# Bucketed attention and two MLPs on one core: four-element reciprocal, GpSimd spreads and value splits, a 128-row bucket-code product, transfers from SyncE

## Chip, cores and metric

One core of a Trainium2 chip runs the whole program. The metric is the device time of one execution in microseconds. Engines are called by the profile's names: PE is TensorE's matmul stream and PEld its weight loads, DVE is VectorE, ACT is ScalarE, POOL is GpSimd, SP is SyncE.

## What is computed

```python
q_bits = (np.einsum('bhsd,dk->bhsk', q, proj) > 0)          # B, H, S, D = 2, 8, 768, 64; 6 bits
mask = q_bucket[:, :, :, None] == k_bucket[:, :, None, :]   # bucket = bits as a number
scores = scale * np.matmul(q, k.transpose(0, 1, 3, 2))
scores = np.where(mask, scores, -1000000000.0)
scores = scores - np.max(scores, axis=-1, keepdims=True)
attn = np.exp(scores)
attn = attn / (np.sum(attn, axis=-1, keepdims=True) + 1e-09)
x = np.matmul(attn, v)                  # heads side by side: 1536 rows of 512
gate = 1.0 / (1.0 + np.exp(-(x @ w_gate)))
x = gate * (x @ w_val) @ w_out          # 512 -> 1536 -> 512
h = x @ w_in                            # 512 -> 2048
g = np.where(h >= 1, h, np.where(h <= -1, 0.0, (h + 1) ** 2 / 4))
out = g @ w_out2                        # 2048 -> 512
```

## The kernel before

The 16 heads are taken as eight pairs (`seq`, L395), the attention of a pair as 12 units (`Unit`): two heads times six tiles of 128 queries. Each unit is one step `kk` of a loop that is written out by hand in `manual_schedule` (L398, L484), so the program's order is the order in each engine's queue. A unit computes scores for 128 queries against 768 keys in PSUM (`QK`, L303, four matmuls), takes the negated row maximum on VectorE (`MAX`, L311), the exponential with its row sum on ScalarE (`EXP`, L315), transposes the 768 columns back through TensorE in pieces of four (`Flip.T`, L341, tile `pt`, two PSUM buffers), and splits each piece into a high f16 part on ScalarE (`HI`, L347) and a low f16 part on VectorE (`LO`, L350). A `pt` buffer is free again only when its `LO` has read it. Every fourth unit closes a group: `ST1` (L318) scales the four row sums, `ST2` (L322) takes their reciprocal on VectorE, spread over 4x64 columns as it is read, into `rb`; two steps later `norm` transposes `rb` on TensorE (L355, tile `r`) and the product with V begins (`pv`, L381, 60 matmuls a group, cut into four pieces). `evac` (L388) multiplies product and reciprocal on VectorE.

V stays exact by a split: `split_v` (L367, L369) makes two residuals of it on VectorE, half a head pair at a time, at steps 1, 3, 5 and 6 of a pair (`VST`, L469); every product with V reads them.

Beside the units of one pair runs the preparation of the next (`Prep`): transposes of q and k (L208, L209, tile `T`), copies and residuals (L212, L216), the hash projections (`z`, L225), their signs (`bits`, L229) and a product with a table of bucket codes (`xp`, L235) that yields a one-hot of the bucket. The table `code` has 56 rows, the signs 56 rows. Five moves between partitions (L281) for each of q and k, and the loads of later q, k and v (`load_qk`, `load_v`), are DMAs from GpSimd's queue, in program order; GpSimd does nothing else in the loop. SyncE issues the first loads and moves and, later, all weights. The last pair has no preparation beside it.

After the attention come the two MLPs, in which TensorE works from weights that SyncE loads (L103).

Of the kernel before, what the change touches and what calls it, by code (L numbers as in the profile page):

```python
# [7 lines left out]
F32 = mybir.dt.float32  # L8
F32R = mybir.dt.float32r
F16 = mybir.dt.float16  # L10
BF16 = mybir.dt.bfloat16
I64 = mybir.dt.int64
U32 = mybir.dt.uint32
AF = mybir.ActivationFunctionType
ALU = mybir.AluOpType
# [11 lines left out]
def lsh_attention_glu_act(ctx, tc, q, k, v, proj, w_gate, w_val, w_out1, w_in2, w_out2, ident_d, code_d, out):  # L27
    nc = tc.nc
# [4 lines left out]
    HN = S // 2  # L33
# [10 lines left out]
    const = ctx.enter_context(tc.tile_pool(name="const", bufs=1))  # L44
# [6 lines left out]
    ZR = 32 + 4 * NB  # L51
    ZW = 72
    Z0 = 32 + 2 * NB
    code_f = const.tile([ZR, 2, 2, 128], F32, name="code_f")
    code = const.tile([ZR, 2, 2, 128], BF16, name="code")
    cst = const.tile([128, 4], F32, name="cst")
    pz = const.tile([128, 2, Z0 + ZW], F32R, name="pz")

    def constants():
        nc.vector.memset(pz.bitcast(F32), 0.0)  # L60
        for i, c in enumerate((-TINY, -2.0 * BIG, -float(NB), 0.5)):
            nc.vector.memset(cst[:, i:i + 1], c)
        nc.scalar.dma_start(ident, ident_d)
        nc.gpsimd.dma_start(proj_sb[E], proj)
        nc.gpsimd.dma_start(proj_sb[O], proj)
        nc.gpsimd.dma_start(code_f, code_d)
        for e, r in ((0, E), (1, O)):
            cs = slice(Z0 + e * NB, Z0 + (e + 1) * NB)
            nc.vector.tensor_copy(pz[r, 0, cs], proj_sb[r])
            nc.vector.tensor_tensor(out=pz[r, 1, cs], in0=proj_sb[r], in1=pz[r, 0, cs].bitcast(F32), op=ALU.subtract)  # L70

    def f(ap):
        return ap.bitcast(F32)
# [77 lines left out]
    with ExitStack() as actx:  # L151
        ap = actx.enter_context(tc.tile_pool(name="attn", bufs=2))
# [1 line left out]
        DMA = nc.gpsimd  # L154
        NAT, PR = {}, {}

        def load_qk(b, p, eng=nc.gpsimd):
            nat = []
            for j, src in enumerate((q, k)):
                t = ap.tile([128, 2, NI * D], F32, tag="nat", bufs=4, name=f"n{j}_{b}_{p}")  # L160
                nat.append(t)
            NAT[b, p] = nat
            eng.dma_start(nat[0], q[b, 2 * p:2 * p + 2].rearrange("h (p i) d -> p h (i d)", i=NI))
            for e in range(2):
                eng.dma_start(nat[1][:, 1 - e], k[b, 2 * p + e].rearrange("(p i) d -> p (i d)", i=NI))

        def load_v(b, p, eng=nc.gpsimd):
            vr = ap.tile([128, 2, NI * D], F32, tag="vr", name=f"vr_{b}_{p}")
            eng.dma_start(vr, v[b, 2 * p:2 * p + 2].rearrange("h (p i) d -> p h (i d)", i=NI))
            VR[b, p] = vr  # L170

        def top(t, i):
            return t.bitcast(BF16).rearrange("p h (s t) -> p h s t", t=2)[:, :, :, i]
# [4 lines left out]
        SG = 4  # L178

        class Prep:  # L180
# [44 lines left out]
                    nc.tensor.matmul(self.z_ps[0:ZW, 0:HN], lhsT=pz[:, c, s:s + ZW], rhs=self.t4[j][t][:, n * HN:(n + 1) * HN], start=(m == 0), stop=(m == len(steps) - 1))  # L225

            def bits(self):
                self.bt = ap.tile([ZR, HN], BF16, tag="bits", bufs=1, name=f"bits_{self.b}_{self.p}")
                nc.scalar.activation(out=self.bt, in_=self.z_ps[0:ZR, 0:HN], func=AF.Sign, bias=cst[0:ZR, 0:1])  # L229

            def xp(self, j, n=None):
                self.x_ps = self.bank(n, f"xp{j}_{self.b}_{self.p}")
                for a in range(2):
                    if n is None or n == a:
                        nc.tensor.matmul(self.x_ps[:, a] if n is None else self.x_ps, lhsT=code[:, a, j, :], rhs=self.bt, start=True, stop=True)  # L235

            def Hot(self, j, dst, r, n=None):
                dst = self.sb(dst, n)[r]
# [38 lines left out]
            def copy(self, j, m):  # L277
                tU, tW, tH, tN = self.t4[j]
                s0, s1 = self.rows(j)
                dst, src = ((tN[O], tU[s0]), (tU[s0], tW[s1]), (tW[s1], tN[O]), (tN[E], tH[E]), (tH[E], tU[s1]))[m]  # L280
                nc.gpsimd.dma_start(f(dst), f(src))  # L281

            def done(self):
                A = [(t[2], t[3]) for t in self.t4]
# [3 lines left out]
        class Unit:  # L288
# [16 lines left out]
            def MAX(self):  # L305
                self.c = self.n % SG
                if self.c == 0:
                    self.st = ap.tile([128, 3, SG], F32, tag="st", bufs=4, name=f"st_{self.u}")
                else:
                    self.st = un[self.n - 1].st  # L310
                nc.vector.tensor_reduce(out=self.st[:, 0, self.c:self.c + 1], in_=self.sc[:, :, 0:HN], op=ALU.max, axis=AX.XY, negate=True)  # L311
# [6 lines left out]
                nc.vector.tensor_scalar(out=self.st[:, 2], in0=self.st[:, 1], scalar1=1e-9, scalar2=PSCALE, op0=ALU.add, op1=ALU.mult)  # L318

            def ST2(self):  # L320
                self.rb = ap.tile([128, 4, 64], F32, tag="rb", name=f"rb_{self.u}")
                nc.vector.reciprocal(out=self.rb, in_=self.st[:, 2].unsqueeze(2).broadcast_to([128, 4, 64]))  # L322

        class Flip:
            def __init__(self, n):
# [34 lines left out]
        def split_v(b, p, h, k):  # L360
            vr = VR[b, p]
            if h == 0 and k == 0:
                VS[b, p] = ap.tile([128, 2, NI * D], F32, tag="vs", name=f"vs_{b}_{p}")
            vs = VS[b, p]
            hs = slice(k, k + 1)
            if h == 0:
                nc.vector.tensor_tensor(out=vs[:, hs], in0=vr[:, hs], in1=top(vr, 1)[:, hs], op=ALU.subtract)  # L367
            else:
                nc.vector.tensor_tensor(out=top(vs, 0)[:, hs], in0=vs[:, hs], in1=top(vs, 1)[:, hs], op=ALU.subtract)  # L369

        def pv(b, p, g, PT):
            vr, vs = VR[b, p], VS[b, p]
# [22 lines left out]
        seq = [(b, p) for b in range(B) for p in range(NP)]  # L395
        UP = 2 * NI

        with tc.manual_schedule():  # L398
            ws0, wraw = [], []

            def load_w(w, t):
                raw = ap.tile([128, 2 * S], I64, tag="PT", bufs=3, name=f"wr_{t}_0")[:, 0:512]
                nc.sync.dma_start(raw.rearrange("p (a n) -> p a n", a=KC), col_chunk(w, 0))
                wraw.append(raw)
# [24 lines left out]
            fw = first_weights()  # L429

            load_qk(*seq[0], nc.sync)
            constants()
            load_w(w_gate, "g")
            load_qk(*seq[1], nc.gpsimd)
            pp, p1 = Prep(*seq[0]), Prep(*seq[1])
            for j in range(2):
                pp.T(j)
# [10 lines left out]
            for j in range(2):  # L448
                pp.swap(j)
            load_v(*seq[0], nc.sync)  # L450
            load_w(w_val, "v")
            nc.vector.tensor_copy(code, code_f)
            pp.bits()
            hold = []
            for j in range(2):
# [28 lines left out]
            for kk in range(-2, NU + DLY + 7):  # L484
# [12 lines left out]
                st = 0 <= kk < NU and kk % SG == SG - 1  # L497
# [28 lines left out]
                if 0 <= pi < len(seq) and m in VST:  # L526
                    split_v(*seq[pi], *VST[m])
# [27 lines left out]
                if nxt and pm == 4 and pj + 2 < len(seq):  # L555
                    load_qk(*seq[pj + 2])
                if 0 <= pi < len(seq) - 1 and m == 9:
                    load_v(*seq[pi + 1])
# [5 lines left out]
                if 0 <= kk - GV0 < 2:  # L564
                    n = kk - GV0
# [165 lines left out]
```

## Time and profile before

| | |
|---|---|
| median of 3 runs | 908.0 us (907.74 to 908.94) |
| the profiled execution | 907.66 us, span 905.8 us |
| busy, share of the span | PE 96%, PEld 87%, DVE 66%, ACT 53%, POOL 6% |
| chain that ended last | PE 70%, DVE 13%, DMA 5%, ACT 5%, issue 5% |
| granted clock of TensorE, mean | 0.987 |

A busy share says how long an engine was occupied, not that it set the pace. Ends of matmuls are modelled, so waits of PE are read best as the distance between the starts of two neighbours, compared with the same two neighbours where nothing held them up. The attention takes the first 330 us of the span, the MLPs the rest.

### The profile page before, as it was taken

To read this page: it belongs to the slowest core of one execution; us is meant where nothing else is said; L and a number is where in the kernel's file an instruction comes from. 1 tells how busy PE (TensorE), PEld (TensorE's weight loads), DVE (VectorE), ACT (ScalarE), POOL (GpSimd) and SP (SyncE) were. 2 spreads that over 40 slices of the span, in tenths; PEclk is the share of its full clock that TensorE was granted. 3 is DMA by queue.
4 is the path that set the end of the run, shared out by engine and by line. 5 is a ranking of instruction groups with operands and counts; after the bars stand their busy time and mean duration, and the time that the engine had idled before them with its cause. 6 is when DMAs were issued, how large, how long until landed. Compare 5 with 4: busy or idle time off the path is not lost.

```text
span 905.8 us, 14442 instructions
## 1 busy us (share of the span) xinstructions
PE 871.1 (96%) x5840; PEld 785.9 (87%) x5840; DVE 601.0 (66%) x1000; ACT 476.8 (53%) x903; POOL 57.0 (6%) x106
## 2 busy tenths in 40 slices
PE   6799999999999889999999999999999999999998
PEld 4587877778777679999999999999999998999996
DVE  4788888888888867453455879599984444444343
ACT  4667677676776654222222435454765555555443
POOL 2212112121111000000000000000000000000000
PEclk9799999999999999999999999999999999999999
DMA  7324323243221005212122543044430001000001
GB/s 211 88 58 106 92 71 97 58 109 89 71 63 45 1 1 164 70 59 81 47 73 87 169 139 118 23 140 149 129 95 1 1 1 43 27 1 1 1 1 71
DMA packets 33811, 64.49 MB, mean 71 GB/s; under 512 B 3060, under 2 KB 24660, under 8 KB 33744
## 3 DMA queue, kind: packets, MB, share of 16 engines
q1 hardware_dynamic: 27616, 41.16, 14.6%
q0 software_dynamic: 5984, 22.34, 9.8%
q8 instruction: 46, 0.75, 0.3%
q14 instruction: 21, 0.17, 0.1%
q10 hardware_dynamic: 144, 0.07, 0.0%
HBM read 45.27 MB, written 3.15 MB: 53 GB/s over the span
## 4 chain that ended last, share of the span: by engine, by line
PE 70%; DVE 13%; DMA 5%; ACT 5%; issue 5%; POOL 1%; SPq 0%; ACTq 0%; POOLq 0%; DVEq 0%
PE p L123 5%; PE p L125 5%; PE p L124 5%; PE o L646 5%; PE o L647 5%; PE o L645 5%; DVE st L311 4%; PE O L381 4%; PE pg L125 4%; PE pg L123 4%; PE pv L123 4%; PE pv L125 4%; PE pv L124 4%; PE pg L124 3%; PE pt L341 3%
## 5 line engine op out<-in xcount | busy, mean ns | idle before, releaser
L350 DVE SCALAR_TENSOR_TENSOR PT<-pt,PT 128x512 f16<-128x512 f32 x144 | 98.5, 684 | 48.5 <-ACT PT L347 48.2
L315 ACT ACTIVATE P<-sc,st 128x768 f32<-128x768 f32 x96 | 86.4, 900 | 49.4 <-DVE st L311 45.8
L341 PE MATMUL pt<-ident,P 128*128 128x128 f32 x576 | 94.4, 284 | 11.1 <-DVE PT L350 10.3
L347 ACT ACTIVATE PT<-pt 128x512 f16<-128x512 f32 x144 | 85.8, 596 | 25.4 <-PE pt L341 25.2
L341 PEld LDWEIGHTS pt<-ident,P 128*128 128x128 f32 x576 | 67.5, 143 | 29.1 <-DVE PT L350 18.1
L311 DVE TENSOR_REDUCE st<-sc 128x1 f32<-128x768 f32 x96 | 89.7, 934 | 0.4 <-PE sc L303 0.4
L381 PE MATMUL O<-PT,vs 128*64 128x256 f16 x864 | 89.2, 279 | 0.0
L123 PE MATMUL p<-yh,wh_i 128*128 128x384 f32 x256 | 86.1, 336 | 0.2 <-DVE yl L602 0.2
L125 PE MATMUL p<-yh,wl_i 128*128 128x384 f32 x256 | 86.0, 336 | 0.0
L124 PE MATMUL p<-yl,wh_i 128*128 128x384 f32 x256 | 85.8, 335 | 0.0
L381 PE MATMUL O<-PT,vr 128*64 128x256 f16 x576 | 75.9, 280 | 2.0 <-ACT x_3h L136 2.0
L647 PE MATMUL o<-wh_o,gl 128*128 128x512 f32 x192 | 75.3, 392 | 0.0
L646 PE MATMUL o<-wl_o,gh 128*128 128x512 f32 x192 | 75.2, 392 | 0.0
L645 PE MATMUL o<-wh_o,gh 128*128 128x512 f32 x192 | 74.7, 389 | 0.0
L629 DVE SCALAR_TENSOR_TENSOR g<-p,t 128x384 f32<-128x384 f32 x64 | 35.4, 553 | 48.3 <-ACT t L627 48.3
L149 DVE SCALAR_TENSOR_TENSOR h<-sg,pv 128x384 f32<-128x384 f32 x48 | 26.4, 550 | 56.2 <-PE pv L125 50.0
L147 ACT ACTIVATE sg<-pg 128x384 f32<-128x384 f32 x48 | 23.4, 487 | 70.2 <-PE pg L125 68.4
L631 DVE TENSOR_TENSOR gl<-g,gh 128x384 fp32r<-128x384 f32 x64 | 35.6, 557 | 31.5 <-ACT gh L630 31.5
L626 ACT ACTIVATE t<-p,cst 128x384 f32<-128x384 f32 x64 | 36.6, 572 | 36.8 <-PE p L125 36.8
L381 PEld LDWEIGHTS <-vs 128*64 128x64 bf16 x864 | 47.4, 112 | 9.8 <-issue 9.5
L630 ACT ACTIVATE gh<-g 128x384 fp32r<-128x384 f32 x64 | 33.6, 525 | 41.9 <-DVE g L629 41.7
L123 PEld LDWEIGHTS p<-yh,wh_i 128*128 128x128 f32 x256 | 48.1, 188 | 1.9 <-DVE yl L602 0.6
(256 smaller groups left out, 2136.7 us busy)
## 6 DMA issues: line engine op xcount, KB each, us to landing
wr_o<-in_moe_w_out_dram SPq DMA_DIRECT2D x28, 512.0 KB, 3.6
wr_i<-in_moe_w_in_dram SPq DMA_DIRECT2D x16, 512.0 KB, 3.7
wr_g<-in_moe_w_gate_dram SPq DMA_DIRECT2D x12, 512.0 KB, 3.7
wr_v<-in_moe_w_val_dram SPq DMA_DIRECT2D x12, 512.0 KB, 4.6
N<-U POOLq DMA_DIRECT2D x15, 192.0 KB, 2.6
n<-in_q_dram POOLq DMA_DIRECT2D x7, 384.0 KB, 4.6
n<-in_k_dram POOLq DMA_DIRECT2D x14, 192.0 KB, 5.1
U<-W POOLq DMA_DIRECT2D x14, 192.0 KB, 3.8
```

The source lines that it names most:

```text
L123: nc.tensor.matmul(ps, lhsT=wh, rhs=rh, start=first, stop=False)
L124: nc.tensor.matmul(ps, lhsT=wh, rhs=rl, start=False, stop=False)
L125: nc.tensor.matmul(ps, lhsT=wl, rhs=rh, start=False, stop=last)
L311: nc.vector.tensor_reduce(out=self.st[:, 0, self.c:self.c + 1], in_=self.sc[:, :, 0:HN], op=ALU.max, axis=AX.XY, negate=True)
L315: nc.scalar.activation(out=self.P, in_=self.sc[:, :, 0:HN], func=AF.Exp, bias=self.st[:, 0, self.c:self.c + 1], scale=1.0, accum_out=self. ...
L341: nc.tensor.transpose(self.ps[m][:, j, :], un[2 * self.n + e].P[:, a, c:c + 128], ident)
L347: nc.scalar.activation(out=self.part(0, m), in_=self.ps[m], func=AF.Copy, scale=PSCALE)
L350: nc.vector.scalar_tensor_tensor(out=self.part(1, m), in0=self.ps[m], scalar=PSCALE, in1=self.part(0, m), op0=ALU.mult, op1=ALU.subtract)
L381: nc.tensor.matmul(O_ps[r, 0:GN], lhsT=vv[m][:, e, i * D:(i + 1) * D], rhs=PT[:, l, e * NI + i, :], start=(s == 0), stop=(s == len(steps) ...
L645: nc.tensor.matmul(oacc[i], lhsT=gh[:, ts], rhs=wh, start=(fc == 0), stop=False)
L646: nc.tensor.matmul(oacc[i], lhsT=gh[:, ts], rhs=wl, start=False, stop=False)
L647: nc.tensor.matmul(oacc[i], lhsT=gl[:, ts], rhs=wh, start=False, stop=(fc == F2 - 1))
```

## The change

The reciprocal is taken of the four sums alone, into a fourth column block of `st`, and GpSimd copies it out to 4x64 columns. The four value splits of a pair go to GpSimd with unchanged operands. `code` and the signs become constant tiles of 128 rows whose rows past 56 are zeroed once by GpSimd, so that the product runs over 128 rows. The defaults of `load_qk` and `load_v`, and the moves, are issued from SyncE; three small loads of constants stay on GpSimd and one on ScalarE.

```diff
-    code = const.tile([ZR, 2, 2, 128], BF16, name="code")
+    code = const.tile([128, 2, 2, 128], BF16, name="code")
+    bt = const.tile([128, HN], BF16, name="bt")
...
+        nc.gpsimd.memset(code, 0.0)
+        nc.gpsimd.memset(bt, 0.0)
...
-        def load_qk(b, p, eng=nc.gpsimd):
+        def load_qk(b, p, eng=nc.sync):
...
-        def load_v(b, p, eng=nc.gpsimd):
+        def load_v(b, p, eng=nc.sync):
...
-                self.bt = ap.tile([ZR, HN], BF16, tag="bits", bufs=1, name=f"bits_{self.b}_{self.p}")
-                nc.scalar.activation(out=self.bt, in_=self.z_ps[0:ZR, 0:HN], func=AF.Sign, bias=cst[0:ZR, 0:1])
+                nc.scalar.activation(out=bt[0:ZR], in_=self.z_ps[0:ZR, 0:HN], func=AF.Sign, bias=cst[0:ZR, 0:1])
...
-                        nc.tensor.matmul(self.x_ps[:, a] if n is None else self.x_ps, lhsT=code[:, a, j, :], rhs=self.bt, start=True, stop=True)
+                        nc.tensor.matmul(self.x_ps[:, a] if n is None else self.x_ps, lhsT=code[:, a, j, :], rhs=bt, start=True, stop=True)
...
-                nc.gpsimd.dma_start(f(dst), f(src))
+                nc.sync.dma_start(f(dst), f(src))
...
-                    self.st = ap.tile([128, 3, SG], F32, tag="st", bufs=4, name=f"st_{self.u}")
+                    self.st = ap.tile([128, 4, SG], F32, tag="st", bufs=4, name=f"st_{self.u}")
...
+                nc.vector.reciprocal(out=self.st[:, 3], in_=self.st[:, 2])
                 self.rb = ap.tile([128, 4, 64], F32, tag="rb", name=f"rb_{self.u}")
-                nc.vector.reciprocal(out=self.rb, in_=self.st[:, 2].unsqueeze(2).broadcast_to([128, 4, 64]))
+                nc.gpsimd.tensor_copy(out=self.rb, in_=self.st[:, 3].unsqueeze(2).broadcast_to([128, 4, 64]))
...
-                nc.vector.tensor_tensor(out=vs[:, hs], in0=vr[:, hs], in1=top(vr, 1)[:, hs], op=ALU.subtract)
+                nc.gpsimd.tensor_tensor(out=vs[:, hs], in0=vr[:, hs], in1=top(vr, 1)[:, hs], op=ALU.subtract)
...
-                nc.vector.tensor_tensor(out=top(vs, 0)[:, hs], in0=vs[:, hs], in1=top(vs, 1)[:, hs], op=ALU.subtract)
+                nc.gpsimd.tensor_tensor(out=top(vs, 0)[:, hs], in0=vs[:, hs], in1=top(vs, 1)[:, hs], op=ALU.subtract)
...
-            load_qk(*seq[1], nc.gpsimd)
+            load_qk(*seq[1], nc.sync)
...
-            nc.vector.tensor_copy(code, code_f)
+            nc.vector.tensor_copy(code[0:ZR], code_f)
```

On VectorE, around the group's end at the middle of the second pair (`st` sums, `PT` the split transposes, `vs` the residuals of V), the queue stood so before:

```order
L350 SCALAR_TENSOR_TENSOR PT_1_0_692<-pt_1_820,PT_1_0_692 128x4x128
L322 RECIPROCAL rb_1_1_1_839<-st_1_0_0_644 128x256
L311 TENSOR_REDUCE st_1_0_2_830<-sc_1_1_2_825 128x1
L350 SCALAR_TENSOR_TENSOR PT_1_0_692<-pt_2_864,PT_1_0_692 128x4x128
L350 SCALAR_TENSOR_TENSOR PT_1_1_874<-pt_0_875,PT_1_1_874 128x4x128
L311 TENSOR_REDUCE st_1_0_2_830<-sc_1_0_3_869 128x1
L369 TENSOR_TENSOR vs_1_749<-vs_1_749 128x384
L350 SCALAR_TENSOR_TENSOR PT_1_1_874<-pt_1_904,PT_1_1_874 128x4x128
```

and stands so now:

```order
L353 SCALAR_TENSOR_TENSOR PT_1_0_696<-pt_1_823,PT_1_0_696 128x4x128
L323 RECIPROCAL st_1_0_0_647<-st_1_0_0_647 128x4
L313 TENSOR_REDUCE st_1_0_2_833<-sc_1_1_2_828 128x1
L353 SCALAR_TENSOR_TENSOR PT_1_0_696<-pt_2_868,PT_1_0_696 128x4x128
L353 SCALAR_TENSOR_TENSOR PT_1_1_878<-pt_0_879,PT_1_1_878 128x4x128
L313 TENSOR_REDUCE st_1_0_2_833<-sc_1_0_3_873 128x1
L353 SCALAR_TENSOR_TENSOR PT_1_1_878<-pt_1_908,PT_1_1_878 128x4x128
```

The reciprocal keeps its place but reads and writes 4 columns in place of 256, and the residual is gone; the neighbours keep their order.

GpSimd's queue in the same pair holds no DMA any more, only the residuals and the spreads:

```order
L370 TENSOR_TENSOR vs_1_753<-vr_1_578 128x384 x2
L325 COPY rb_1_1_1_843<-st_1_0_0_647 128x256
L372 TENSOR_TENSOR vs_1_753<-vs_1_753 128x384 x2
L325 COPY rb_1_1_3_1004<-st_1_0_2_833 128x256
L325 COPY rb_1_1_5_1191<-st_1_0_4_996 128x256
```

The first two residuals stand ahead of the pair's first spread, the other two ahead of its second.

SyncE's queue at the start, with names as above (`n` the loads of q and k, `B`, `N`, `H`, `U`, `W` the prepared operands of a pair):

```order
L406 DMA wr_g_96<-in_moe_w_gate_dram 128x4x128
L166 DMA n_0_1_98<-in_q_dram 128x2x384
L168 DMA n_0_1_99<-in_k_dram 128x384 x2
L255 DMA B_122<-U_0_0_103 64x768
L255 DMA N_0_0_127<-U_0_0_124 64x768
L255 DMA B_145<-U_0_0_124 64x768
L255 DMA H_0_0_126<-U_0_0_124 64x768
L268 DMA U_0_0_103<-W_0_0_104 64x768
L268 DMA U_0_0_124<-W_0_0_125 64x768
L172 DMA vr_0_187<-in_v_dram 128x2x384
L406 DMA wr_v_189<-in_moe_w_val_dram 128x4x128
L283 DMA N_0_1_152<-U_0_1_149 64x768 x2
```

The three `n_0_1` loads stood on GpSimd's queue and now stand ahead of the first pair's moves; the second pair's first move `N_0_1` now stands behind them and two loads.

## Rows read from the trace of the kernel before

**Rows 1.** Windows: stretch, length, busy us (instructions) PE PEld DVE ACT POOL, clock, DMA, GB/s.
```profile
36.00:40.00 4.00, 1.57 (x7) 1.40 (x7) 4.00 (x6) 2.47 (x5) 0.26 (x1) 0.85 0.25 59
40.00:44.00 4.00, 3.52 (x13) 2.23 (x11) 2.99 (x6) 2.44 (x5) 0.26 (x1) 0.50 0.23 49
165.31:203.08 37.77, 36.37 (x352) 29.57 (x348) 31.74 (x48) 26.37 (x55) 7.78 (x15) 1.00 0.33 84
278.63:316.40 37.77, 34.43 (x340) 27.17 (x334) 32.53 (x47) 23.67 (x49) 0.25 (x1) 1.00 0.06 16
420.00:905.80 485.80, 481.25 (x2584) 456.40 (x2582) 288.69 (x518) 228.97 (x417) 0.00 (x0) 1.00 0.20 63
```

**Rows 2.** Waits of PE (total, times, longest): 52 to 278.5 us, then 278.5 to 321.
```profile
PE pt L341 <- DVE PT L350: 4.8, 12, 0.6
PE T L208 <- DVE W L216: 3.1, 6, 0.6
...
PE pt L341 <- DVE PT L350: 3.7, 7, 0.9
```

**Rows 3.** Chain in order of time (start, us, what): steady pair, last pair.
```profile
191.49 1.66 DVE rb L322
...
197.12 0.50 DVE vs L369
...
278.71 1.66 DVE rb L322
```

**Rows 4.** Timeline of PE in the steady pair: start, us, line, operation, [idle <-releaser].
```profile
171.54 0.33 PE L208 MATMUL T<-ident,n 128*128 128x128 f32 x1 [0.54 <-DVE W L216]
...
182.20 0.51 PE L225 MATMUL z<-W,pz 128*72 128x384 f32 x2
182.55 0.60 PE L341 MATMUL pt<-ident,P 128*128 128x128 f32 x4
...
185.61 0.44 PE L355 MATMUL r<-ident,rb 128*128 128x128 f32 x2
185.88 0.60 PE L341 MATMUL pt<-ident,P 128*128 128x128 f32 x4
...
188.44 0.33 PE L235 MATMUL xp<-bits,code 56*128 56x384 bf16 x1
188.70 0.66 PE L341 MATMUL pt<-ident,P 128*128 128x128 f32 x4
...
194.08 0.33 PE L235 MATMUL xp<-bits,code 56*128 56x384 bf16 x1
194.61 0.93 PE L341 MATMUL pt<-ident,P 128*128 128x128 f32 x4 [0.19 <-DVE PT L350]
...
197.21 0.44 PE L355 MATMUL r<-ident,rb 128*128 128x128 f32 x2
198.25 0.66 PE L341 MATMUL pt<-ident,P 128*128 128x128 f32 x4 [0.61 <-DVE PT L350]
```

**Rows 5.** Groups by line, shapes apart, 0 to 400 us, VectorE.
```profile
L350 DVE SCALAR_TENSOR_TENSOR PT<-pt,PT 128x512 f16<-128x512 f32 x144 | 98.5, 684 | 48.5 <-ACT PT L347 48.2
...
L322 DVE RECIPROCAL rb<-st 128x256 f32<-128x256 f32 x24 | 41.8, 1741 | 0.0
...
L369 DVE TENSOR_TENSOR vs<-vs 128x384 bf16<-128x384 f32 x16 | 9.3, 584 | 0.0
...
L367 DVE TENSOR_TENSOR vs<-vr 128x384 f32<-128x384 f32 x16 | 8.8, 548 | 0.0
...
L318 DVE TENSOR_SCALAR st<-st 128x4 f32<-128x4 f32 x24 | 3.8, 159 | 0.0
```

**Rows 6.** Issues of DMAs: count, KB each, median us to landing.
```profile
vr<-in_v_dram POOLq DMA_DIRECT2D x7, 384.0 KB, 3.6
...
vr<-in_v_dram SPq DMA_DIRECT2D x1, 384.0 KB, 4.7
```

## The prediction

> **What bounds the kernel now.** I read the windows first, to split the span by stage. From 420 us to the end PE is busy 481.25 of 485.80 us at full clock [rows 1]: that is the MLP half, which the change doesn't touch, and nothing is to be had there. The attention repeats every 37.77 us, one head pair, with PE at 36.37 and DVE at 31.74 us busy; the last pair, which prepares no successor, takes as long with PE at 34.43 us [rows 1]. So PE is nearly full, but not quite, and the reader should ask what it waits for. The waits of PE answer that: in six pairs it idles 4.8 us for `LO` to free a `pt` buffer and 3.1 us for the residual W, and in the last pair 3.7 us for `LO` [rows 2]. All of these are DVE instructions. The chain in order of time shows why DVE is late: a reciprocal of 1.66 us stands in it, and in the same pair a value residual of 0.50 us; in the last pair four reciprocals stand in it, of which the row is the first [rows 3]. The kernel is held by PE in most of a pair, and by DVE around the ends of the groups.
>
> How much PE loses there I take from the distances of starts, since ends of matmuls are modelled [rows 4]. From `r` to `pt` it is 198.25 - 197.21 = 1.04 us where PE waited, and 185.88 - 185.61 = 0.27 where it didn't: 0.77 lost. From `xp` to `pt` 0.53 against 0.26: 0.27. The four transposes at 194.61 take 0.93 against 0.66 at 188.70: 0.27. T at 171.54 waited 0.54. Together 1.85 us a pair. Six pairs make 11.1 us, where the waits count 7.9; with the same factor of 1.4 the last pair's 3.7 become 5.2.
>
> **Reciprocal and spread.** Removed: 24 instructions of 1.741 us [rows 5], 1.66 of them on the chain each time. Added on DVE: 24 on four elements. The nearest row is `ST1` on the same four sums, 0.159 us, of which 0.08 stands in the queue before its successor starts; I take 0.08. DVE gets 1.58 us back at each group's end. Added on POOL: 24 copies of 128x256. No row has one. Its duration lies between nothing and, as the nearest row, the 1.741 us that DVE took for as many columns; what counts is whether it ends in time, and the transposes of `rb` come late: DVE's reciprocal ends at 191.49 + 1.66 = 193.15 and PE reads `rb` at 197.21 [rows 3, 4]. That leaves 4.06 us, plus the 1.58 by which it starts earlier, less the 0.54 us (0.27 twice) that PE gains between: about 5 us. I cost the copy at nothing, covered by the units between; if it took over 5 us, PE would wait for the rest in every group.
>
> **Value splits.** Removed from DVE: 32 of 0.55 or 0.58 us [rows 5], four a pair; on the chain a residual is worth 0.50 [rows 3]. Added on POOL: the same, at a price between DVE's own 0.58 us and, as a bound, four times that. POOL does nothing else then, and the first two of a pair need only V in place, so that they run ahead of where DVE had them; PE first reads them late in the pair. I cost them at nothing. The Trainium skill, GPSIMD Engine Reference (section Elementwise — side-by-side cycle accounting), gives about 2.6 cycles an element for a two-input operation, an estimate of 0.83 us for 384 elements; the sum would be the same.
>
> **What the relief is worth.** A reciprocal and up to two residuals leave each of the places where PE waited: at least 1.58 us of DVE against losses of at most 0.77 us each. The W that holds T follows a reduction that follows a reciprocal, so that wait goes too. What is late next is PE itself: 37.77 - 1.85 = 35.9 us of its own work a pair, where DVE falls to 31.74 - 3 x 1.58 - 4 x 0.57 = 24.7 us. I let nine tenths of the loss go, since `LO` also waits for `HI` on ACT (48 us in all [rows 5]) and some of that may surface: 0.9 x (11.1 + 5.2) = 14.7 us. The first pair has two reciprocals and four splits among the weight conversions, 2 x 1.58 + 4 x 0.5 = 5.2 us of DVE at most, 0 at least; PE runs there partly at half clock (0.50 [rows 1]) and can use less, so I take 2.0.
>
> **The padded product.** The matmuls, 28 of them in the loop, keep their 384 columns. After `xp` the next transposes start 0.26 us later, while after `z` it is (182.55 - 182.20)/2 = 0.175 a matmul [rows 4]: 0.085 us that 56 rows or bf16 may cost. The saving is between 0 (were it the type, which stays) and 28 x 0.085 = 2.4 us; I take the middle, 1.2, as the row cannot say which. The Trainium skill, TensorEngine Tiling (Array Packing), section Key Properties, says that a change of tiling mode drains TensorE, and 56 rows need a half-height mode, 128 don't. By that rule the full 2.4 us go and the time is 1.2 us lower; the gap in the row agrees with it, without excluding the type.
>
> **Transfers on SyncE.** 99 DMAs (71 moves, 21 loads of q and k, 7 of V) go from one queue to the other in the same order. The load of V landed after 3.6 us from POOL and after 4.7 in the single case from SP, in the crowded start [rows 6]. Even 1.1 us more is small against the slack of V, which is loaded a third of a pair (12 us) ahead. Two zero fills go ahead of POOL's three small loads at the start. I cost all this at nothing, between a gain of half a microsecond (the first moves share the engines with one queue fewer) and a loss of one, if the second pair's loads hold up the first pair's moves; the cover is the slack, and without it each late move would hold a `QK`.
>
> **The sum.** 14.7 + 2.0 + 1.2 = 17.9 us. The profiled execution took 907.66 us, 0.34 under the median; 907.7 - 17.9 = 889.8, for a median about 890. Own range of this case: 885 (all losses gone, 2.4 for the product, 3 more in the first pair) to 895 (a third of the losses stay).
>
> **Rivals.**
> *Half of it comes back as a wait for ScalarE.* `LO` idles 48 us for `HI` [rows 5]; if the exponential and `HI` set the pace once DVE is free, about half of the 16.3 us stay. For it: that idle time stands in every group. Against it: ACT is busy 26.37 of 37.77 us [rows 1], and its waits are for DVE's reduction. Time: 907.7 - 8 - 1.2, or 898 (895 to 901).
> *The early stretch also gets its clock back.* From 40 to 44 us the granted clock is 0.50, the lower level, after four microseconds in which PE was busy for 1.57 and DVE for 4.00 [rows 1]. With DVE faster there, PE may stay at its upper level; if the stretch at half clock is 8 us long (an estimate, twice the row), this gives back at most half of it: 886 (883 to 887).
> *Slower: POOL blocks DVE.* If a DVE instruction cannot run while POOL computes, DVE loses POOL's whole time. It decides from 7.0 us of POOL a pair (3 x 1.58 + 4 x 0.57 removed). With splits at twice 0.58 and spreads at 1.74, POOL takes 9.8: DVE is 2.8 us worse a pair, half of it on the path, eight pairs: +11, or 919 (912 to 926). Against it: the spread has no division, and the instructions that matter (`LO`, the reduction, W) read PSUM. The Trainium skill, SBUF — State Buffer, section Who interferes with whom, states that VectorE and GpSimd share a port pair by an exclusive lock, but that a VectorE instruction with at most one SBUF input, outside the two-port modes, doesn't contend. By that rule the loop's instructions are free and only the weight conversions of the first pair and the four-element ones could block; no row of before has both engines computing.
> *Nothing changes.* PE may be held by its own order, and the waits may only move. Against it: they end with DVE rows. 907 to 909.
>
> **How the numbers follow.** Chances: forecast 0.56, half 0.20, clock 0.12, blocked 0.07, nothing 0.05. Predicted 890.0, the likeliest's. The range 883 to 900 holds the forecast and the clock case and most of the half case, and leaves out about 0.15 to 0.2. A measurement tells 0.2% (1.8 us) from no change: faster 0.88, same 0.05, slower 0.07.
>
> **What would show it.** Right: the reciprocal near 0.1 us, `LO` no longer a releaser of `pt` in PE's waits, pairs 35.4 to 36.2 us apart, POOL's copy ending long before `r`, `xp` to `pt` 0.17 to 0.26. Wrong: pairs over 37 us, PE waiting at `r` for POOL or at `QK` for a move, or reductions longer than 0.95 us where POOL computes.

## The result, and the profile after

The changed kernel takes 884.14 us (median of 4 runs, 883.65 to 885.9) where the kernel before took 907.87 (907.2 to 908.94): a ratio of 0.9741, 95% interval 0.9724 to 0.9758. It is faster by 23.7 us, where 17.9 were forecast; 890.0 was predicted, in a range of 883 to 900. The profiled execution of the changed kernel took 885.9 us and is the slowest of its four, so against the profiled 907.66 us of before there are 21.8 us to place.

The busy times are those of the profile's page.

```profile
PE 860.6 (97%) x5840; PEld 785.5 (89%) x5840; DVE 554.9 (63%) x968; ACT 473.6 (54%) x903; POOL 38.0 (4%) x65
```

The windows (columns as in [rows 1]) of a steady pair, and from 420 us to the end:

```profile
158.00:193.48 35.48, 35.48 (x349) 29.67 (x347) 25.96 (x44) 25.93 (x55) 4.34 (x7) 1.00 0.35 89
420.00:884.10 464.10, 458.88 (x2457) 434.26 (x2455) 277.63 (x496) 222.80 (x406) 0.00 (x0) 1.00 0.20 63
```

A pair is 35.48 us long instead of 37.77, and PE is busy in all of it, where it was busy for 36.37 of 37.77 [rows 1]. DVE went from 31.74 to 25.96 us a pair, POOL takes 4.34. The stretch behind the attention is as full as it was. The waits of PE, first from 0 to 60 us, then from 60 to 320 us, where this row is the only one:

```profile
PE T L211 <- DMA n<-in_q_dram: 6.2, 2, 4.5
...
PE pt L344 <- DVE PT L353: 1.3, 3, 0.6
```

```profile
PE O L384 <- DVE xr L391: 1.7, 1, 1.7
```

The waits for `LO` and for W [rows 2] are gone; the row that is left stands in the last pair. The chain that ended last, from 180 to 196 us, holds no DVE piece any more, where before the reciprocal and a residual stood in it [rows 3]:

```profile
by line: PE O L384 38.0%; PE sc L305 27.7%; PE pt L344 26.4%; PE xp L237 6.2%; PE r L358 2.3%
```

Groups by line, with `LO` and the reciprocal as in [rows 5], and POOL's new work:

```profile
L353 DVE SCALAR_TENSOR_TENSOR PT<-pt,PT 128x512 f16<-128x512 f32 x144 | 99.3, 690 | 64.4 <-ACT PT L350 64.3
L313 DVE TENSOR_REDUCE st<-sc 128x1 f32<-128x768 f32 x96 | 90.6, 943 | 0.2 <-PE sc L305 0.2
L323 DVE RECIPROCAL st<-st 128x4 f32<-128x4 f32 x24 | 4.1, 169 | 0.0
...
L370 POOL TENSOR_TENSOR vs<-vr 128x384 f32<-128x384 f32 x16 | 13.3, 854 | 16.5 <-DMA vr<-in_v_dram 16.5
L372 POOL TENSOR_TENSOR vs<-vs 128x384 bf16<-128x384 f32 x16 | 12.9, 831 | 0.0
L325 POOL COPY rb<-st 128x256 f32<-128x256 f32 x24 | 9.5, 398 | 249.6 <-DVE st L323 183.3 <-PE O L384 66.2
```

The reciprocal fell from 1741 to 169 ns. `LO` waits longer for `HI` than before (64.4 us, 48.5 in [rows 5]), and this costs nothing there, since from 60 us on PE no longer waits for `LO`. The timeline of one group's end shows how early POOL's copy is:

```profile
183.25 0.40 POOL L325 COPY rb<-st 128x256 f32<-128x256 f32 x1 [11.04 <-PE O L384]
...
183.60 1.62 POOL L372 TENSOR_TENSOR vs<-vs 128x384 bf16<-128x384 f32 x2
...
188.15 0.44 PE L358 MATMUL r<-ident,rb 128*128 128x128 f32 x2
```

It ends at 183.65, 4.5 us before PE transposes `rb`.

To see where time goes in every run, I cut each profiled execution at the starts of the maxima (the 96 DVE reductions, one a unit, 12 units a pair; the first has number 0): the start of the first, from there to number 8, a pair (the mean of the six up to number 80, without the first or the first two where these still differ), from number 80 to the last, and from the last to the end. The last column is the mean granted clock of that execution. All in us:

| kernel | first | 0 to 8 | a pair | 80 to last | to the end | clock |
|---|---|---|---|---|---|---|
| before | 18.09 | 32.36 | 37.77 | 42.76 | 585.9 | 0.987 |
| after | 19.66 | 30.36 | 35.49 | 36.72 | 584.4 | 0.989 |
| recip_alone | 18.99 | 27.22 | 35.99 | 37.56 | 583.3 | 0.995 |
| split_alone | 18.29 | 32.55 | 37.54 | 41.38 | 584.2 | 0.989 |
| pad_alone | 18.72 | 32.50 | 37.78 | 42.78 | 585.0 | 0.985 |
| dma_alone | 18.88 | 32.49 | 37.79 | 42.79 | 585.9 | 0.985 |
| no_pad | 17.62 | 26.75 | 36.00 | 36.69 | 584.3 | 0.996 |
| no_split | 18.22 | 28.61 | 35.63 | 37.79 | 583.9 | 0.996 |
| no_dma | 17.91 | 27.15 | 35.49 | 36.68 | 583.4 | 0.998 |
| n1_pool | 17.66 | 26.74 | 35.50 | 36.69 | 584.0 | 0.998 |
| n1_first | 17.43 | 26.79 | 35.49 | 36.68 | 585.1 | 0.998 |
| pool_load | 17.90 | 30.39 | 35.81 | 37.82 | 584.4 | 0.990 |
| pad64 | 18.13 | 30.08 | 36.00 | 36.68 | 584.5 | 0.989 |
| pad72 | 19.52 | 26.75 | 35.49 | 36.70 | 584.7 | 0.998 |

From before to after the first maximum is 1.57 us later, the next eight units are 2.00 shorter, the six pairs 13.7, the last pair 6.0 and the rest 1.5: 21.6 us. The pairs repeat to 0.02 us where the kernel is steady, so this column tells parts apart that the medians cannot: runs of one and the same kernel differ by several us, with the granted clock. In one session the kernel before ran from 902.7 to 909.2 us, at mean clocks between 0.984 and 0.994.

### The profile page after: what moved, and what is told of

It reads as the page before. It is cut to its first block, busy times and chain, and to the rows that moved or that the text cites. A ratio compares the mean times of both kernels' runs of the same rounds, so it can differ in the third digit from the quotient of the medians.

```text
span 884.1 us, 14495 instructions
## 1 busy us (share of the span) xinstructions
PE 860.6 (97%) x5840; PEld 785.5 (89%) x5840; DVE 554.9 (63%) x968; ACT 473.6 (54%) x903; POOL 38.0 (4%) x65
## 4 chain that ended last, share of the span: by engine, by line
PE 94%; DVE 2%; ACT 2%; DMA 1%; issue 0%; SPq 0%; DVEq 0%; ACTq 0%
PE O L384 10%; PE sc L305 7%; PE pt L344 7%; PE p L126 5%; PE p L128 5%; PE p L127 5%; PE o L649 5%; PE o L650 5%; PE o L648 5%; PE y L126 4%; PE y L127 4%; PE y L128 4%; PE pg L128 4%; PE pv L128 4%; PE pg L126 4%; PE pv L127 4%
## 5 line engine op out<-in xcount | busy, mean ns | idle before, releaser
L353 DVE SCALAR_TENSOR_TENSOR PT<-pt,PT 128x512 f16<-128x512 f32 x144 | 99.3, 690 | 64.4 <-ACT PT L350 64.3
L344 PE MATMUL pt<-ident,P 128*128 128x128 f32 x576 | 89.7, 278 | 1.4 <-DVE PT L353 1.3
```

What stands on the lines that cost most here:

```text
L344: nc.tensor.transpose(self.ps[m][:, j, :], un[2 * self.n + e].P[:, a, c:c + 128], ident)
L353: nc.vector.scalar_tensor_tensor(out=self.part(1, m), in0=self.ps[m], scalar=PSCALE, in1=self.part(0, m), op0=ALU.mult, op1=ALU.subtract)
```

## The experiments: one part alone

My theory was that the long reciprocal sets off all the stalls, that the splits come second, and that padding and queue move little. The rivals were that reciprocal and splits are needed together, that the padding counts in full by itself, and that the queue brings a gain. Each part was put alone into the kernel before.

**Reciprocal alone.**

```
+ nc.vector.reciprocal(out=self.st[:, 3], in_=self.st[:, 2])
- nc.vector.reciprocal(out=self.rb, in_=self.st[:, 2].unsqueeze(2)...)
+ nc.gpsimd.tensor_copy(out=self.rb, in_=self.st[:, 3].unsqueeze(2)...)
```

> The kernel before with only the reciprocal changed (four sums, spread by a copy on GpSimd). Theory A: the stalls of a pair are all set off by the 1.66 us reciprocal, the copy on GpSimd (about 0.4 us) hides, and the splits alone are too short to stall TensorE: 13 to 15 us go in the steady pairs and 5 to 6 in the last, 888 to 891 us against 907.9. Theory B: reciprocal and split add up, and half of the stalls stay for the split: 896 to 900 us. Rival C: the wait for the copy costs as much as it gives: 905 to 909 us.

887.57 us (884.98 to 889.69), a ratio of 0.9788 [0.9757, 0.9819]. A pair takes 35.99 us, so 1.78 of the 1.85 us that [rows 4] gave as lost are gone, and the last pair is 5.2 shorter, with its splits still on DVE. The waits of PE from 52 to 330 us name `LO` twice, and W not at all:

```profile
PE pt L342 <- DVE PT L351: 0.6, 2, 0.4
```

Theory A, though the steady pairs gave less than the 13 to 15 us that it named: six times 1.78 are 10.7 us. The reciprocal alone carries 1.78 of the 2.28 us by which the whole change shortens a pair.

**Splits alone.**

```
- nc.vector.tensor_tensor(out=vs[:, hs], in0=vr[:, hs], ...)
+ nc.gpsimd.tensor_tensor(out=vs[:, hs], in0=vr[:, hs], ...)
(and the second one alike)
```

> The kernel before with only the value splits moved to GpSimd. Theory A: VectorE's chain over the stalled stretch of a pair is shorter by the splits in it, about 0.5 to 1 us a pair, so 3 to 7 us of the whole: 901 to 905 us. Theory B: the reciprocal alone makes the stalls and the splits fill idle time: 907 to 908.5 us. Rival C: GpSimd's two-input reads hold VectorE back: slower than 909 us.

904.8 us (10 runs, 900.63 to 906.29), 0.9972 [0.9952, 0.9992]. A pair is 37.2 to 37.75 us, 0.2 us less in the mean, and the last one 1.4 shorter. PE still waits for both, from 52 to 330 us:

```profile
PE T L208 <- DVE W L216: 3.5, 6, 0.6
PE pt L341 <- DVE PT L350: 2.6, 8, 0.4
```

Against [rows 2], `LO` is better (2.6 here in the six pairs and the last together, 4.8 and 3.7 before) and W isn't. The time lies in theory A's range, but against the kernel before in the same session (907.1 us) the gain is 2.3 us, a little under the 3 that it began at. So theory A, weakly: removing the smaller piece from DVE shortens the stall at places where a split stands, and leaves those of the reciprocal.

**Padding alone.**

```
- code = const.tile([ZR, 2, 2, 128], BF16, name="code")
+ code = const.tile([128, 2, 2, 128], BF16, name="code")
+ bt = const.tile([128, HN], BF16, name="bt")
(zeroed once; the product reads all 128 rows)
```

> The kernel before with only the bucket-code product padded to 128 rows. The products should be spaced 0.09 us closer at two of the three steps around each of their places, some 0.36 us a pair. Theory A: they lie in the stretch where TensorE waits for VectorE, so the saved time turns into waiting: 907 to 908 us. Theory B: it comes off the time in full, 2.2 us: 905.5 to 906 us. Rival C: the two memsets delay the start: 908.5 to 909.5 us.

905.85 us (10 runs), 0.9995 [0.9975, 1.0015]. The bare time would fit theory B, but the kernel before took 907.1 us in the same session and the interval spans no change; the pair decides, and it stays at 37.78 us: theory A. The timeline shows where the gain went:

```profile
194.60 0.34 PE L237 MATMUL xp<-bt,code 128*128 128x384 bf16 x1
...
195.41 0.93 PE L343 MATMUL pt<-ident,P 128*128 128x128 f32 x4 [0.47 <-DVE PT L352]
```

PE is done sooner with the product and waits 0.47 us for `LO`, where it waited 0.19 [rows 4]. Its waits for `LO` from 52 to 330 us add up to 10.8 us, 8.4 before: 2.4 us more, which is what 28 products of 0.085 us were to save. A gain on PE in a stretch that DVE sets turns into waiting.

**SyncE issuing alone.**

```
- nc.gpsimd.dma_start(f(dst), f(src))
+ nc.sync.dma_start(f(dst), f(src))
(also the loads of q, k and V)
```

> The kernel before with only the DMA issues moved from GpSimd's queue to SyncE's. Theory A: the second pair's loads now stand behind the gate weights on one queue and TensorE waits for them at about 11 us, 1.6 to 2 us longer in the first 12 us; part of it comes back by unit 8: 908 to 910 us. Theory B: the transfers land as before or are hidden: 907.5 to 908.3 us. Rival C: steady transfers that are issued earlier shorten the pairs: 903 to 906 us.

907.08 us (10 runs), 1.0008 [0.9988, 1.0028]; a pair of 37.79 us. The steady moves are worth nothing on either queue. The first maximum is 0.8 us later than before (0.6 with the padding alone), and the time is that of the kernel before in the same session (907.1): theory B, and theory A's wait isn't borne out by this run.

## The experiments: one part taken back

Since padding was worth nothing by itself, the parts don't add. So each was also taken out of the changed kernel.

**Without padding** (the diff above, reversed).

> The changed kernel without the padding (56 rows again). Theory A: the padding is worth nothing while TensorE waits for VectorE and its full 0.36 to 0.43 us a pair once it doesn't: a pair 35.49 becomes 35.85 to 35.95 us, the whole 2 to 2.6 us longer, 886 to 887. Theory B: it is worth as little here as it was alone: a pair 35.5 us, the whole 884 to 884.5.

885.2 us (883.17 to 888.43) at granted clocks that happened to be higher; the pair decides: 36.00 against 35.49 us, 0.51 us or 3.0 in six pairs. Theory A, and more than expected. The timelines of a product and the flip behind it (`Flip.T`, the four transposes of a piece into `pt`), without and with padding:

```profile
176.29 0.33 PE L235 MATMUL xp<-bits,code 56*128 56x384 bf16 x1
176.56 0.66 PE L342 MATMUL pt<-ident,P 128*128 128x128 f32 x4
```

```profile
180.42 0.34 PE L237 MATMUL xp<-bt,code 128*128 128x384 bf16 x1
180.59 0.60 PE L344 MATMUL pt<-ident,P 128*128 128x128 f32 x4
```

The start of the flip comes 0.27 us behind the product without padding and 0.17 with it, and the four flips behind it take 0.66 against 0.60. Four of the eight steps around the four products of a pair are 0.09 us shorter (0.36), and three groups of flips 0.055 (0.16): 0.52, the 0.51 measured. The other four steps, those next to the products with V (128x64), take the same with either height: 0.21 us before a code product, 0.27 behind one.

**64 and 72 rows.** The same tiles at two other heights:

```
- code = const.tile([128, 2, 2, 128], BF16, name="code")
+ code = const.tile([64, 2, 2, 128], BF16, name="code")
(bt alike; 72 in the other run)
```

> The changed kernel with the code product on 64 rows in place of 128. Theory A: the price is that of a product of at most half the array's height between full ones: at 64 rows it is there as at 56, a pair 36.0 us, 0.264 us from a code product to the flip behind it. Theory B: any zero rows up to the next multiple of 32 are enough: 35.5 us and 0.173 us.

> The changed kernel with the code product on 72 rows in place of 128. Theory A: over half the array's height is as good as the full height: a pair 35.5 us, 0.173 us from a code product to the flip behind it. Theory B: only the full 128 rows are free: 36.0 us and 0.264 us, or something between by the rows that are missing.

64 rows: 887.1 us (2 runs), a pair of 36.00. 72 rows: 883.2 us (2 runs), a pair of 35.49.

```profile
180.13 0.33 PE L237 MATMUL xp<-bt,code 64*128 64x384 bf16 x1
180.40 0.66 PE L344 MATMUL pt<-ident,P 128*128 128x128 f32 x4
```

```profile
176.69 0.34 PE L237 MATMUL xp<-bt,code 72*128 72x384 bf16 x1
176.86 0.60 PE L344 MATMUL pt<-ident,P 128*128 128x128 f32 x4
```

64 rows behave as 56, and 72 as 128: both theories A. It is neither the type nor zero rows as such, but the step between 64 and 72 rows. The Trainium skill, TensorEngine Tiling (Array Packing), section Key Properties, says that a change of tiling mode drains TensorE, and its section When to Use Tiling puts contractions of up to 64 in a mode of half the rows. The runs agree in the step between 64 and 72 rows and give its price here, 0.09 us at four of eight steps and 0.055 in the group behind; that it is a drain, no row shows by itself.

**Splits back on VectorE** (the diff above, reversed).

> The changed kernel with the value splits back on VectorE. Theory A: without the long reciprocal, VectorE keeps up with the splits too, but for up to 1 us in the last pair, which is denser: a pair 35.5 us, the whole 884 to 885.5. Theory B: the splits cost what they gave alone, 0.3 us a pair and 2 to 3 us in all: 886 to 887.

885.7 us (885.03 to 887.09). A pair of 35.63 us, 0.14 more, and the last 1.07 more, so 1.9 us in all: between the theories, nearer to A. PE waits 0.6 us for `LO` in two places again. So the splits are worth 1.9 us beside the short reciprocal and the padding, and 2.8 beside the long reciprocal (1.4 in six pairs, 1.4 in the last). Beside the short reciprocal without padding they are worth 0.9: `recip_alone` and `no_pad` differ by them and by the queue of the transfers, and a pair takes 35.99 and 36.00 us there, the last one 37.56 and 36.69.

**All DMAs back on GpSimd.**

```
- nc.sync.dma_start(f(dst), f(src))
+ nc.gpsimd.dma_start(f(dst), f(src))
(also the loads of q, k and V, those of the second pair too)
```

> The changed kernel with all the DMA issues back on GpSimd's queue, those of the steady pairs too. Theory A: of the moved issues only the first loads of the second pair count, and they count against the change: 879.5 to 881, like the run that put these loads alone back, a pair 35.5 us. Theory B: the steady issues wait on GpSimd behind the splits, tiles of the next pair come late and TensorE waits: a pair 35.7 us or more, 881 to 886.

882.57 us (879.94 to 884.25), a pair of 35.49. The steady issues are worth nothing here either, theory B is out; two of the four runs, 879.94 and 881.06 us, are at theory A's time or within 0.1 us of it, the other two are 3 us above.

## The experiments: the start

In the profiled execution after, TensorE's second wait for q was long:

```profile
10.96 0.30 PE L211 MATMUL T<-ident,n 128*128 128x128 f32 x1 [1.77 <-DMA n<-in_q_dram]
```

The load stands behind 512 KB of gate weights on SyncE's queue. Two edits undo this in two ways.

**Second pair's loads on GpSimd** (`n1_pool`), and **ahead of the weights** (`n1_first`):

```
- load_qk(*seq[1], nc.sync)
+ load_qk(*seq[1], nc.gpsimd)
```

```
  constants()
+ load_qk(*seq[1], nc.sync)
  load_w(w_gate, "g")
- load_qk(*seq[1], nc.sync)
```

> The changed kernel with the first loads of the second pair issued by GpSimd again, past the gate weights on SyncE's queue. Theory A: the order on the queue makes TensorE's second wait of 1.8 us at 11 us; it falls below 0.4 us, the whole 882 to 883. Theory B: what bounds that landing is the sum of the transfers of the first 10 us, whichever queue holds them: a wait between 0.2 and 1.8 us as in the other runs, the whole within 0.7 us of 884.

> The changed kernel with the second pair's loads ahead of the gate weights on SyncE's queue. Theory A: what counts is that the second pair's q lands by about 9 us, whichever queue it is on: no second wait, the first maximum at 17.5 to 17.9 us instead of 19.7, little half clock, 879.5 to 881. Theory B: the gate weights, some 1.5 us later, then hold up VectorE's work on them and the start: first maximum at 18.5 us or later, 883 to 886.

`n1_pool`: 879.73 us (879.39 to 879.94), 0.9708 [0.9674, 0.9742], below what either theory allowed; the wait is 0.20:

```profile
9.24 0.30 PE L211 MATMUL T<-ident,n 128*128 128x128 f32 x1 [0.20 <-DMA n<-in_q_dram]
```

`n1_first`: 880.92 us (880.19 to 886.1), no second wait at all, and a first maximum at 17.43 us. Both fit the order on the queue as the cause. But other runs speak against it as the whole cause: with these loads on GpSimd the wait was 1.60 us in `recip_alone`, whose queues are those of before, and with them behind the weights it was 0.28 in `no_pad` and 0.33 in `dma_alone`, and there was no second wait in `pad64` and `pool_load`:

```profile
10.01 0.30 PE L208 MATMUL T<-ident,n 128*128 128x128 f32 x1 [1.60 <-DMA n<-in_q_dram]
```

So the wait lies between nothing and 1.8 us behind the weights and between 0.2 and 1.6 on GpSimd's queue, and a single profile of each can't separate queue from chance.

Much of what differs behind the first maximum is the granted clock. Windows of before, after and `n1_pool`, over the same times but for the last row of the first two, which shows the same work, the passage to the MLPs, 20.2 us earlier after the change:

```profile
18.00:28.00 10.00, 7.11 (x29) 5.64 (x28) 4.17 (x6) 3.41 (x7) 2.34 (x4) 0.52 0.45 126
28.00:38.00 10.00, 7.42 (x44) 5.70 (x42) 8.86 (x16) 6.46 (x13) 2.26 (x4) 0.97 0.45 116
38.00:49.00 11.00, 9.29 (x32) 6.77 (x32) 8.91 (x12) 7.58 (x17) 1.56 (x3) 0.54 0.17 36
328.00:333.00 5.00, 4.43 (x52) 3.95 (x54) 3.99 (x6) 2.00 (x3) 0.00 (x0) 0.66 0.01 3
```

```profile
18.00:28.00 10.00, 7.16 (x26) 5.92 (x27) 6.06 (x8) 2.90 (x6) 2.05 (x2) 0.53 0.53 142
28.00:38.00 10.00, 9.61 (x50) 7.86 (x48) 6.33 (x10) 6.66 (x13) 0.00 (x0) 0.79 0.47 129
38.00:49.00 11.00, 7.53 (x48) 5.81 (x46) 8.19 (x14) 8.13 (x18) 1.97 (x3) 0.84 0.20 43
307.80:312.80 5.00, 4.67 (x67) 4.48 (x68) 3.74 (x5) 2.02 (x3) 0.00 (x0) 1.00 0.01 3
```

```profile
18.00:28.00 10.00, 6.75 (x47) 5.80 (x46) 7.22 (x10) 6.10 (x12) 1.95 (x2) 1.00 0.61 178
28.00:38.00 10.00, 6.58 (x36) 4.94 (x35) 7.36 (x14) 7.18 (x16) 1.98 (x3) 0.88 0.36 80
38.00:49.00 11.00, 10.13 (x91) 8.26 (x91) 8.45 (x14) 8.11 (x17) 0.40 (x1) 0.95 0.36 93
```

In the first, PE was at half its clock for most of 18 to 28 and of 38 to 49 us; in the second for most of 18 to 28 and part of what follows; in the third the clock stays at 1.00 up to 28 us, and only a few us after are at the lower level. PE issues 47 matmuls from 18 to 28 us there and 26 in the second. In the table, 0 to 8 takes 26.7 to 28.6 us at mean clocks of 0.995 and more, 30 to 32.6 at lower ones. The same kernel draws both: `no_dma` took 879.94 us at 0.998 and 884.25 at 0.989. The four timed runs of the changed kernel were all at 0.989 to 0.992 and those of `n1_pool` all at 0.997 or 0.998, which is in favour of the earlier load, but the kernel before was also faster in that session (905.65 against 907.87). Whether the load's place makes the higher clock likelier stays open.

The late load does not bring the low clock by itself. `pad72` has the queues of the changed kernel, a second wait of 1.48 us and its first maximum at 19.52 us (19.66 there), but takes 26.75 us for the next eight units instead of 30.36, with the clock at 1.00 where the changed kernel had 0.53:

```profile
18.00:28.00 10.00, 6.33 (x41) 5.51 (x42) 7.40 (x10) 4.72 (x10) 2.05 (x2) 1.00 0.69 195
```

`n1_pool` is the fastest version that was run; its interval overlaps that of the changed kernel.

## The experiment on the shared port

**More work on GpSimd.** One instruction a unit beside VectorE, with nothing reading its output:

```
+ nc.gpsimd.tensor_tensor(out=dum[:, 1], in0=dum[:, 0],
+     in1=self.st[:, 0, self.c:self.c + 1].broadcast_to([128, 384]), op=ALU.mult)
```

> The changed kernel with one more instruction on GpSimd for each of the 96 units, a product of two SBUF operands of 128x384 f32 into a buffer that nothing reads, ordered behind the unit's maximum; about 0.85 us each, 80 us in all. Theory A: GpSimd's reads don't hold VectorE's instructions, which have at most one SBUF operand in this stretch: evictions 0.69 us, maxima 0.94 us as before, the whole 884 to 885. Theory B: GpSimd shuts VectorE out while it reads: VectorE's instructions that overlap it are longer by 0.2 to 0.8 us, stalls on the evictions return, 890 to 905.

887.69 us (887.59 to 888.38), a pair of 35.81, 0.32 more. Between the theories, so the groups and the timeline decide. Groups from 60 to 300 us, then a stretch where the engines overlap, then another:

```profile
L356 DVE SCALAR_TENSOR_TENSOR PT<-pt,PT 128x512 f16<-128x512 f32 x124 | 85.5, 689 | 56.7 <-ACT PT L353 56.6
L315 DVE TENSOR_REDUCE st<-sc 128x1 f32<-128x768 f32 x83 | 78.2, 943 | 0.0
...
L323 DVE TENSOR_SCALAR st<-st 128x4 f32<-128x4 f32 x21 | 6.1, 290 | 0.0
```

```profile
146.51 0.69 DVE L356 SCALAR_TENSOR_TENSOR PT<-pt,PT 128x512 f16<-128x512 f32 x1
...
147.11 0.17 DVE L326 RECIPROCAL st<-st 128x4 f32<-128x4 f32 x1
...
146.68 0.83 POOL L316 TENSOR_TENSOR dum<-dum,st 128x384 f32<-128x384 f32 x1 [4.17 <-DVE st L323]
```

```profile
133.19 0.83 POOL L316 TENSOR_TENSOR dum<-dum,st 128x384 f32<-128x384 f32 x1 [3.67 <-DVE st L315]
133.43 0.62 DVE L323 TENSOR_SCALAR st<-st 128x4 f32<-128x4 f32 x1
```

`LO` and the maxima are as long as in the changed kernel (690 and 943 ns), also where GpSimd computes beside them: theory A for these. But `ST1`, on four elements, took 0.62 instead of 0.16 us, six times from 60 to 300 us, each time begun while GpSimd computed and ended with it to 0.03 us (133.43 + 0.62 = 134.05, and 133.19 + 0.83 = 134.02). That is theory B, for this one instruction. It is not the size that decides: the reciprocal, on four elements too, kept its 0.17 us in all fourteen places from 60 to 300 us where it began while GpSimd computed, as at 147.11. PE also waits for the splits now, 1.9 us in seven places from 60 to 320 us, since they stand behind the new instructions on GpSimd; from the third pair on that is 0.21 of the 0.32 us that a pair lost. How the rest divides between `ST1` and other causes wasn't traced, nor why the last pair is 1.1 us longer. The Trainium skill, SBUF — State Buffer, section Who interferes with whom, says that a VectorE instruction in a two-port mode and one of GpSimd shut each other out for the whole instruction, that the form of `ST1` can be in such a mode, and that instructions with one SBUF input outside these modes don't contend. The rows agree with the first by `ST1`'s end, 0.03 us behind GpSimd's, and with the last by `LO`, the maxima and the reciprocal; in which mode `ST1` ran, no row shows.

## Why the prediction was right, and where it was off

The mechanism was right, and most sizes were off. The forecast's own range was 885 to 895, and 884.14 lies below it, at a time that the clock rival had (883 to 887) and whose mechanism the profile after doesn't show; its lower end adds up, by the terms named for it, to 907.7 - 16.3 - 2.4 - 5.0 = 884.0 and not 885. That the wide range from 883 held the result is in part luck: three terms were too small, one was too large and 1.5 us stood in no term, and had the first pair given the 2.0 us that were taken for it, the time would have been about 882.5.

**What bounds the kernel.** Right: the waits and the chain led to the reciprocal, and with it alone nearly all the stalls went.

**Reciprocal and spread.** Right. The short reciprocal takes 0.169 us, of which 0.08 stands in the queue before the maximum behind it starts (182.92 to 183.00), as the sum had it. The copy takes 0.398 us and is 4.5 us early, where 5 were worked out.

**Value splits.** Right that they hide. They take 0.83 to 0.85 us on GpSimd, between the bounds; an estimate of 0.83 by the Trainium skill, GPSIMD Engine Reference, section Elementwise — side-by-side cycle accounting, agrees. They are worth 1.9 us on top of the reciprocal and the padding, and 0.9 on top of the reciprocal alone.

**What the relief is worth: under-sized.** "I let nine tenths of the loss go" was the step. 10.0 us were taken for six pairs and 10.7 went with the reciprocal alone; 4.7 for the last pair, and 6.0 went. Of these 6.0, the reciprocal alone gave 5.2, the whole loss as worked out, and the splits with the rest 0.8 more. So the loss was sized right (1.78 of 1.85 us a pair) and the nine tenths were not: ScalarE did not take over.

**The first pair: over-sized.** 2.0 us were taken and 0.4 came by the eighth unit, 1.57 us being lost before the first maximum.

**The padded product: under-sized.** 1.2 us were taken, the middle between type and mode; 3.0 came in the six pairs. It was the height and not the type, in full, and the flips behind the product gain too, which the row had shown (0.66 here, 0.60 behind a full product [rows 4]) and the step left out. And it counts only because the reciprocal went: alone it gave nothing.

**Transfers.** Right for the pairs: nothing. The bound of one us lost at the start was passed by the first maximum in the profiled execution (1.57); how much of it is the queue is open.

**Not in the sum.** 1.5 us between the last maximum and the end. Before, the clock fell to 0.50 for a while around 330 us (0.66 in the window above), just after some two microseconds in which PE idled (busy for 1.03 from 326 to 329 us); after, the same work has 1.00. In the three profiled runs that show this fall (before, `pad_alone`, `dma_alone`) the stretch takes 585.0 to 585.9 us, in the others 583.3 to 585.1, so the two groups overlap and the fall need not be the whole of the 1.5 us. What brings it about is open: the three have the longest last pair (42.8 us), but `split_alone`, with 41.4 and stalls of 2.1 us for `LO`, has no fall.

Together: 10.7 + 3.0 + 6.0 + 0.4 + 1.5 = 21.6 us against 17.9; the median gained some 2 us more, the profiled execution being the slowest of four.

**Rivals.** ScalarE as the next bound: `LO` idles more for it, PE never does. GpSimd in VectorE's way: 4.34 us a pair, below the 7.0 from which it was to decide, and being held is seen in a conversion of the first pair (line 103, 1.20 us beside the first splits, 0.69 in `no_dma`) and, with more work on GpSimd, in `ST1`, not in the loop's large instructions. The clock in the early stretch: it does come back in runs of variants, worth up to 3.6 us from the first maximum to the eighth unit (26.7 to 26.8 us against 30.36), but not in the profiled run of the change.

## What to carry to other kernels

When one long instruction of a helper engine stands in the chain at each place where the main engine stalls, removing it can pay nearly the whole of the stalls (1.78 of 1.85 us a pair here); work them out from distances of starts in the timeline, not from wait rows alone, which counted 7.9 us where 10.7 went. A gain on the main engine in a stretch that another engine sets is worth nothing until that engine is relieved, so judge such edits by taking them out of the final kernel, not by adding them to the first. Where runs differ by the clock of one stretch, compare a steady period of the trace (here 12 units, equal to 0.02 us) rather than the medians.

## What the hardware did that I had not expected

A matmul of 64 rows between full ones cost 0.09 us at four of the eight steps around it in a pair and 0.055 us in the group behind, one of 72 rows nothing. `ST1`, an instruction of VectorE on four elements, took 0.62 instead of 0.16 us beside a GpSimd instruction and ended with it, while the reciprocal on four elements and the large ones that read PSUM were not held at all. And two kernels that differ only in the rows of one product, 72 and 128, took 26.75 and 30.36 us for the same eight units, with the granted clock at 1.00 and 0.53 in the first of these stretches; neither height holds the pairs up, so the clock is the likely cause, though each has one profile.
